# The weights of a two-layer block brought in in longer runs, four neighbouring rows to a partition

## The chip, the cores and the metric

The kernel runs on one core of one Trainium2 chip. The metric is the device time of one execution in microseconds; three runs of the kernel before are given below, and one further execution was taken with the hardware profiler.

## What is computed

A gated linear recurrence over 768 steps for 4 batches of 8 heads of 48 columns, and behind it a block of two matrix products with a gate between them:

```python
for t in range(S):                                  # S = 768, D = 48
    state = alpha[:, :, t, :, None] * state + np.einsum('bhd,bhe->bhde', k[:, :, t], v[:, :, t])
    y[:, :, t] = np.einsum('bhd,bhde->bhe', q[:, :, t], state)
x = y.transpose(0, 2, 1, 3).reshape(B * S, H * D)   # 3072 x 384
h = x @ w_in                                        # 384 x 2048
out = (h * np.cos(h)) @ w_out                       # 2048 x 384
```

Inputs and output are fp32; the kernel calculates its products in bf16. The change touches only how `w_in` and `w_out` lie in SBUF.

## The kernel before

The 3072 tokens are worked on in 12 pairs J of two 128-token chunks, three pairs to a batch. For each pair the recurrence is done in chunked form: logarithms of alpha (`ln`), their running sums by matmul (`cums0`, `cums`), exponentials (`icp`, `exps`), scaled k and q (`sk`, `sq`, into kh and qh), transposes (`trans`, into T_ps and qkT), scores, mask, the state between chunks (`outer`, `add`, `state`), and the transposed output (`yT`, evicted into xT). Then the two products follow. `m1` (`mlp1`) calculates h for four tiles of 128 of the 2048 middle columns at a time, u = 0 to 3, each tile f with three matmuls over the 384 rows of the first weights; `sin` makes the cosine on ACT and `gate` multiplies on DVE into gsb, where tile ft = 4u + f has its 128 middle columns on the partitions. `m2` (`mlp2`) sums gsb times the second weights over all 16 tiles, in four parts, into o_ps.

Both weights stay in SBUF for the whole kernel, as bf16: w1 with 128 partitions x 3 x 2048, w2 with 128 partitions x 16 x 384. They are brought in by eight transfers issued from POOL, which convert from fp32 on the way: `load_w1(u)` brings 512 columns, in runs of 2048 bytes of the source, and `load_w2(u)` brings 512 rows, in runs of 1536 bytes, row 128a + p of the block on partition p at place a. The inputs q, k, v and alpha are loaded by SP, and SP writes the results out. The loads of alpha of pair 2 wait for the last matmul of yT of pair 1 (`GATES` and `AFTER`), and all loads that stand behind it in SP's queue wait with it.

The order of all work is written out by hand: `PLAN` gives each step of each pair a planned time in ns, a step may name its engine (`:A`, `:D`), and the steps are issued sorted by these times. Only the order counts; each engine takes its own instructions in that order and waits where data is missing. `IDLE` puts in matmuls on zeros, "fillers", at some times in the start phase, so many at each.

Of the kernel before, what the change touches and what calls it, by code (L numbers as in the profile page):

```python
# [16 lines left out]
def kernel(  # L17
# [10 lines left out]
    nc = tc.nc  # L28
    B, H, S, D = q.shape
    DM, DF = moe_w_in.shape  # L30
    C = 128
# [8 lines left out]
    FW = 4  # L40
# [53 lines left out]
    w1 = consts.tile([C, KT, DF], BF, tag="w1", name="w1")  # L94
# [22 lines left out]

    WQ = FW * C

    def load_w1(u):  # L120
        nc.gpsimd.dma_start(
            out=w1[:, :, u * WQ : (u + 1) * WQ],
            in_=moe_w_in[:, u * WQ : (u + 1) * WQ].rearrange("(kk p) f -> p kk f", p=C),
        )

    def load_w2(u):
        nc.gpsimd.dma_start(
            out=w2[:, FW * u : FW * (u + 1)],
            in_=moe_w_out[u * WQ : (u + 1) * WQ, :].rearrange("(a p) d -> p a d", p=C),
        )  # L130

    act_now = [None]
# [221 lines left out]
    def mlp1(J, u):  # L354
        h_ps[J, u] = ps.tile([C, FW, T2], FP, tag="h", name="h_ps", bufs=3)
        for f in range(FW):
            ft = u * FW + f
            for kk in range(KT):
                nc.tensor.matmul(h_ps[J, u][:, f, :], w1[:, kk, ft * C : (ft + 1) * C], xT[J][:, kk, :],  # L359
                                 start=(kk == 0), stop=(kk == KT - 1))  # L360

    def cosine(J, u):
# [47 lines left out]
    def idle(n):  # L410
# [18 lines left out]


    PLAN = {
# [66 lines left out]
    }  # L498
    IDLE = [(1201, 12), (6413, 16), (11874, 2), (13039, 6), (14889, 9), (17476, 6)]

    order = []
    for key, line in PLAN.items():
        kind, *rest = key.split()
        for J, word in enumerate(line.split()):
            if word != "-":
# [39 lines left out]
```

## Time and profile before

| | |
|---|---|
| median of 3 runs | 187.04 us (187.01 to 188.32) |
| profiled execution | 186.2 us, of which its span is 184.4 us |
| granted TensorE clock | 1.00 |
| TensorE busy | 177.7 us, 96% of the span |
| VectorE, ScalarE, GpSimd busy | 72%, 69%, 45% |
| transfers of the first weights | 4 of 384 KB written, 7.6 us from issue to landing |
| transfers of the second weights | 4 of 384 KB written, 9.2 us |

In the lines of the profile, PE is TensorE's matmuls and PEld its weight loads, which run beside the matmuls; DVE is VectorE, ACT ScalarE, POOL GpSimd, SP the engine that issues most transfers. L359 is line 359 of the kernel before, the matmul of `mlp1`; L388 that of `mlp2`; L167 the matmul in `cums` with two moving columns; L121 and L127 are the two weight transfers. A group's line gives its tiles and shapes, the number of instructions, busy us, the mean ns of one, and behind the bar its engine's idle time before it and what ended that. A line of the waits gives who waited for whom, the us in total, how often, and the longest. A line of the chain gives start, length and what. Matmuls are pipelined, so the time from one to the next is read from the chain and not from the duration of one. In the DMA view a line of a queue gives packets, MB written and the time that its packets took as a share of all 16 DMA engines; q0 is POOL's queue, which carries the weights, and q1 is SP's.

### The profile page before, as it was taken

The page shows a single profiled execution, that of the slowest core. Times are in us where ns is not written, and L with a number is a line of the kernel's source. Part 1 is how long each engine was busy: PE and PEld are TensorE (multiplying, and loading weights), DVE is VectorE, ACT ScalarE, POOL GpSimd, SP SyncE. Part 2 cuts the span into 40 slices and gives each one's busy share as a digit, 9 for nine tenths or more (in the row PEclk, how much of TensorE's full clock was granted, in tenths as well). Part 3 has the DMA queues.
Part 4 walks back from the last instruction along what each step waited for, and adds up shares of the span by engine and source line. Part 5 has one row for each costly group of instructions (what it writes and reads, how often), then busy time and mean ns, then how long its engine had stood idle before and what let it go on. Part 6 is the DMA issues. An engine that isn't in the chain of part 4 may idle for free.

```text
span 184.4 us, 5780 instructions
## 1 busy us (share of the span) xinstructions
PE 177.7 (96%) x2478; PEld 127.1 (69%) x2480; DVE 132.6 (72%) x176; ACT 127.1 (69%) x166; POOL 83.9 (45%) x116
## 2 busy tenths in 40 slices
PE   7999999899999999999999999999999999999993
PEld 2455687565687776876778668676777786787772
DVE  7367673559889799899548986886979769352651
ACT  2572887899889987779787999637945163372720
POOL 5379830297765693943874189492600121000000
PEclk9999999999999999999999999999999999999999
DMA  5999999999999969968968893050420204010212
GB/s 148 261 261 192 187 203 247 237 271 264 257 197 242 310 174 279 226 158 202 301 151 211 202 304 72 0 132 14 116 73 4 60 5 170 4 43 4 85 43 85
DMA packets 60137, 29.47 MB, mean 160 GB/s; under 512 B 51024, under 2 KB 60112, under 8 KB 60112
## 3 DMA queue, kind: packets, MB, share of 16 engines
q1 hardware_dynamic: 56256, 25.86, 57.6%
q0 software_dynamic: 3712, 3.15, 11.1%
q8 instruction: 19, 0.31, 0.7%
q10 hardware_dynamic: 144, 0.10, 0.2%
q14 instruction: 6, 0.05, 0.1%
HBM read 25.17 MB, written 4.72 MB: 162 GB/s over the span
## 4 chain that ended last, share of the span: by engine, by line
PE 76%; ACT 10%; DMA 7%; DVE 2%; issue 1%; SPq 1%; ACTq 0%
PE h_ps L359 29%; PE o_ps L388 27%; DMA a<-in_alpha_dram 7%; PE y_ps L338 5%; PE A_ps L272 3%; PE T_ps L258 3%; PE idle_ps L414 3%; ACT lna L141 2%; DVE gsb L370 2%; PE U_ps L289 2%; ACT c_sb L365 2%; ACT xT L349 2%; PE o_last L382 1%; ACT L136 1%; ACT L365 1%
## 5 line engine op out<-in xcount | busy, mean ns | idle before, releaser
L370 DVE TENSOR_TENSOR gsb<-h_ps,c_sb 128x1024 bf16<-128x1024 f32 x48 | 58.1, 1221 | 24.1 <-ACT c_sb L365 23.2
L365 ACT ACTIVATE c_sb<-h_ps,halfpi 128x1024 bf16<-128x1024 f32 x48 | 53.1, 1115 | 23.5 <-PE h_ps L359 23.1
L359 PE MATMUL h_ps<-xT,w 128*128 128x256 bf16 x576 | 67.6, 273 | 0.6 <-DVE gsb L370 0.3
L388 PE MATMUL o_ps<-w,gsb 128*128 128x384 bf16 x368 | 66.5, 326 | 0.0
L359 PEld LDWEIGHTS <-w 128*128 128x128 bf16 x576 | 55.5, 98 | 9.5 <-issue 0.9
L388 PEld LDWEIGHTS <-gsb 128*128 128x128 bf16 x368 | 34.1, 98 | 20.7 <-issue 0.2
L277 DVE TENSOR_TENSOR A_sb<-A_ps,msk 128x1024 bf16<-128x1024 f32 x24 | 29.0, 1216 | 3.6 <-PE A_ps L272 3.6
L311 POOL TENSOR_TENSOR un<-us,c 128x384 bf16<-128x384 f32 x20 | 16.7, 837 | 30.0 <-DVE us L303 27.4
L212 POOL TENSOR_TENSOR kh<-k,icp 128x384 bf16<-128x384 f32 x22 | 21.8, 1002 | 14.6 <-ACT icp L192 14.6
L216 POOL TENSOR_TENSOR qh<-q,cp 128x384 bf16<-128x384 f32 x16 | 16.6, 1043 | 0.8 <-DMA q<-in_q_dram 0.8
L149 POOL TENSOR_TENSOR a<-a 128x384 f32<-128x384 f32 x9 | 9.0, 1000 | 15.7 <-DMA a<-in_alpha_dram 15.7
L264 DVE COPY qkT<-T_ps 128x1024 bf16<-128x1024 bf16 x18 | 11.8, 680 | 5.0 <-PE T_ps L258 4.8
L414 PE MATMUL idle_ps<-zeros 128*128 128x512 bf16 x49 | 12.9, 412 | 1.4 <-DVE zeros L52 1.2
L349 ACT CAST xT<-y_ps 128x384 bf16<-128x384 f32 x17 | 9.0, 599 | 5.6 <-PE y_ps L338 5.0
L219 POOL CAST vp<-v 128x768 bf16<-128x768 f32 x12 | 10.2, 854 | 5.7 <-DMA v<-in_v_dram 5.7
L141 ACT ACTIVATE lna<-a 128x768 bf16<-128x768 f32 x12 | 10.1, 843 | 3.5 <-DMA a<-in_alpha_dram 3.5
L136 ACT ACT_TABLE_LOAD x9 | 11.5, 1283 | 0.9 <-PEq L529 0.7
L365 ACT ACT_TABLE_LOAD x9 | 11.5, 1283 | 0.2
L303 DVE TENSOR_TENSOR us<-U_ps,un 128x384 f32<-128x384 f32 x16 | 8.7, 550 | 2.7 <-POOL un L311 2.5
L400 ACT COPY o_sb<-o_ps 128x384 f32<-128x384 f32 x11 | 5.2, 476 | 7.2 <-PE o_ps L388 7.2
L414 PEld LDWEIGHTS <-zeros 128*128 128x128 bf16 x51 | 4.8, 105 | 7.3 <-issue 2.2
L264 ACT COPY qkT<-T_ps 128x1024 bf16<-128x1024 bf16 x6 | 6.0, 1014 | 5.3 <-PE T_ps L258 5.1
(70 smaller groups left out, 159.7 us busy)
## 6 DMA issues: line engine op xcount, KB each, us to landing
a<-in_alpha_dram SPq DMA_DIRECT2D x12, 384.0 KB, 5.9
q<-in_q_dram SPq DMA_DIRECT2D x12, 384.0 KB, 5.7
k<-in_k_dram SPq DMA_DIRECT2D x12, 384.0 KB, 5.9
v<-in_v_dram SPq DMA_DIRECT2D x12, 384.0 KB, 5.6
out_dram<-o_sb SPq DMA_DIRECT2D x23, 192.0 KB, 3.0
vs<-vp SPq DMA_DIRECT2D x36, 64.0 KB, 2.9
w<-in_moe_w_in_dram POOLq DMA_DIRECT2D x4, 384.0 KB, 7.6
w<-in_moe_w_out_dram POOLq DMA_DIRECT2D x4, 384.0 KB, 9.2
```

The source lines that it names most:

```text
L136: nc.scalar.preload_act_table_set("natural_log_exp_and_others")
L141: nc.scalar.activation(out=lna_t[J % NL][:, :, :, 0:D].rearrange("p e h d -> p h e d"), in_=a_sb.pop(J), func=AF.Ln)
L212: eng.tensor_tensor(out=kh_t[J % NQ][:, e, :, 0:D], in0=kqv["k", J][:, :, e], in1=icp_, op=ALU.mult)
L216: eng.tensor_tensor(out=qh_t[J % NQ][:, e, :, 0:D], in0=kqv["q", J][:, :, e], in1=cp, op=ALU.mult)
L264: copy(out=qkT_sb[J][:, c], in_=T_ps[J][:, c].rearrange("r n e s -> r n (e s)"))
L277: nc.vector.tensor_tensor(out=A_sb[J][:, c].rearrange("s a p t -> s (a p) t"), in0=A_ps.pop((J, c)).rearrange("s a p t -> s (a p) t"), in1 ...
L311: nc.gpsimd.tensor_tensor(out=u, in0=U_sum.pop(n), in1=c2_sb[J][:, :, c].unsqueeze(3).to_broadcast([C, NP, 2, D]), op=ALU.mult)
L359: nc.tensor.matmul(h_ps[J, u][:, f, :], w1[:, kk, ft * C : (ft + 1) * C], xT[J][:, kk, :], start=(kk == 0), stop=(kk == KT - 1))
L365: nc.scalar.activation(out=c_sb[J, u], in_=h_ps[J, u], func=AF.Sin, bias=halfpi, scale=1.0)
L370: nc.vector.tensor_tensor(out=gsb[J][:, u * FW : (u + 1) * FW], in0=h_ps.pop((J, u)), in1=c_sb.pop((J, u)), op=ALU.mult)
L388: nc.tensor.matmul(o_ps[J, c][:, 0:DM], gsb[J][:, ft, c * C : (c + 1) * C], w2[:, ft], start=(ft == 0), stop=(ft == NF - 1))
L414: nc.tensor.matmul(idle_ps[0], zeros[:, 0:C], zeros, start=True, stop=True)
```

## The change

The second weights lie otherwise in SBUF: of each block of 512 rows, partition p now takes the four neighbouring rows 4p to 4p + 3, which is one run of 6144 bytes of the source. So that gsb's partitions fit to it, tile f of block u must hold the middle columns 4c + f of the block, c = 0 to 127, and the weight loads of L359 read the columns of w1 four apart. The first weights keep their place in SBUF and are brought in by two transfers of 1024 columns, in runs of 4096 bytes; the steps "w1" 2 and 3 are empty. `PLAN` has new times and one of the fillers is gone.

```diff
     def load_w1(u):
-        nc.gpsimd.dma_start(
-            out=w1[:, :, u * WQ : (u + 1) * WQ],
-            in_=moe_w_in[:, u * WQ : (u + 1) * WQ].rearrange("(kk p) f -> p kk f", p=C),
-        )
+        if u < 2:
+            cols = slice(2 * u * WQ, 2 * (u + 1) * WQ)
+            nc.gpsimd.dma_start(out=w1[:, :, cols], in_=moe_w_in[:, cols].rearrange("(kk p) f -> p kk f", p=C))

     def load_w2(u):
         nc.gpsimd.dma_start(
             out=w2[:, FW * u : FW * (u + 1)],
-            in_=moe_w_out[u * WQ : (u + 1) * WQ, :].rearrange("(a p) d -> p a d", p=C),
+            in_=moe_w_out[u * WQ : (u + 1) * WQ, :].rearrange("(p a) d -> p a d", a=FW),
         )
...
     def mlp1(J, u):
         h_ps[J, u] = ps.tile([C, FW, T2], FP, tag="h", name="h_ps", bufs=3)
         for f in range(FW):
-            ft = u * FW + f
             for kk in range(KT):
-                nc.tensor.matmul(h_ps[J, u][:, f, :], w1[:, kk, ft * C : (ft + 1) * C], xT[J][:, kk, :],
+                cols = w1[:, kk, u * WQ : (u + 1) * WQ].rearrange("p (c a) -> p a c", a=FW)[:, f]
+                nc.tensor.matmul(h_ps[J, u][:, f, :], cols, xT[J][:, kk, :],
                                  start=(kk == 0), stop=(kk == KT - 1))
...
-        "w1": "13130 11430 15880 12280",
-        "w2": "19161 17541 20961 22950",
+        "w1": "11430 12280 13180 13181",
+        "w2": "18455 16835 20255 22800",
...
-    IDLE = [(1201, 12), (6413, 16), (11874, 2), (13039, 6), (14889, 9), (17476, 6)]
+    IDLE = [(1201, 12), (6413, 16), (11874, 2), (13039, 6), (14889, 8), (17327, 6)]
```

The other times of `PLAN` are new as well, mostly by less than 1 us. Engine by engine, the order of the instructions is the same as before except for two things: POOL issues six weight transfers instead of eight, and TensorE has one filler fewer, ahead of the transposes T_ps of pair 1.

128 rows, old and new, of the table PLAN are left out of this document.

## The prediction, made before the changed kernel was run

> **What bounds the kernel now.** I read the page's busy shares first, then the chain that ended last, then the waits, and then went into the one stretch in which the weights are brought in.
>
> ```profile
> PE 177.7 (96%) x2478; PEld 127.1 (69%) x2480; DVE 132.6 (72%) x176; ACT 127.1 (69%) x166; POOL 83.9 (45%) x116
> PEclk9999999999999999999999999999999999999999
> ```
> TensorE is busy for 177.7 of 184.4 us at the full clock; no other engine is above 72%. A busy share can hide stalls inside, so the waits of TensorE alone, from 20 us to 181.5 us, are the better measure:
>
> ```profile
> PE cums_h L155 <- ACT lna L141: 0.8, 1, 0.8
> PE T_ps L258 <- DVE gsb L370: 0.3, 1, 0.3
> PE h_ps L359 <- DVE gsb L370: 0.3, 1, 0.3
> ```
> That is all: 1.4 us in 161 us. Behind 20 us nothing that makes another engine or a transfer quicker can bring more than 1.4 us. What can cost much is anything that makes a matmul slower, since there is no idle time to take it up. The chain in order of time shows the pace of the two sorts of matmul that matter (start, length, what), first in the start phase and then late:
>
> ```profile
> 26.71 6.89 DMA a<-in_alpha_dram
> 33.60 0.02 issue
> 33.62 0.85 ACT lna L141
> ...
> 98.41 0.08 PE cums L167 x4
> ...
> 148.44 3.93 PE h_ps L359 x36
> ```
> 36 matmuls of L359 take 3.93 us: 109 ns each, for 256 columns. Four of L167 take 0.08 us: 20 ns each, and eight in another place 0.18 us, 23 ns each. L167 streams 2 columns behind a full 128x128 weight load, so a full load from consecutive columns holds up the matmul behind it for no more than about 23 ns. The first line is the only transfer on the chain behind 10 us: the load of the third pair's alpha, which is held back to the end of yT of pair 1 and then needs 6.89 us.
>
> **The change, part by part.**
>
> *1. The weight loads of L359 read every fourth column.* 576 loads that read 256 bytes of a partition in one run now pick 128 columns out of 1024 bytes. The trace has no strided weight load. The nearest rows are these (all loads of TensorE by shape):
>
> ```profile
> L359 PEld LDWEIGHTS <-w 128*128 128x128 bf16 x576 | 55.5, 98 | 9.5 <-issue 0.9 <-DVE gsb L370 0.2
> L338 PEld LDWEIGHTS <-vs 128*32 128x32 bf16 x384 | 6.0, 97 | 0.0
> L234 PEld LDWEIGHTS <-ident_bf 64*64 64x64 bf16 x12 | 0.7, 103 | 0.9 <-issue 0.5
> ```
> All records are near 98 ns, whether 32 or 128 columns are read, so a record is mostly a latency that the next matmul does not wait out; what counts is the 23 ns. Lower bound: the stride costs nothing (a gain is excluded, because the matmul behind is already at its streaming pace of 109 ns). Upper bound for a load that is still pipelined: four times the stretch read, four times the time, 4 x 23 = 92 ns. A load runs under the 256-column matmul before it, and 92 is below 109, so within a group of 12 both bounds give 0. They differ at the first load of a group. Of the 48 groups, 13 follow o_ps (163 ns a matmul, hidden) and 22 follow another group of L359; the other 13 follow short matmuls of 20 to 41 ns, and there a load may show by up to 92 - 23 = 69 ns: 13 x 69 = 0.9 us. I take twice the consecutive price, 46 ns, since half of what is read is the nearer case to the row: 13 x 23 = +0.3 us, range 0 to +0.9.
>
> A rule of the Trainium skill bears on it (SBUF — State Buffer, the note on cachelines in the section Door 1: The DMA port swizzle): accesses that hit the same 16-byte line twice or more run at full bandwidth, and each crossing to a new line pays a penalty whose size is not given. Four bf16 columns are 8 bytes, so each line is still hit twice and by the first half the load is free, by the second it crosses four times as often; no row here shows which, and the sum by the first half would be 0.3 us lower.
>
> *2. First weights in two transfers, not four; the second weights in longer runs.* The DMA engines are full from 14 us to 30 us with weights alone (two windows of the DMA view, 14 to 30 us and 30 to 34 us):
>
> ```profile
> DMA packets 3655, 3.13 MB, mean 196 GB/s; under 512 B 181, under 2 KB 3652, under 8 KB 3652
> q0 software_dynamic: 3584, 3.06, 123.9%
> ...
> q1 hardware_dynamic: 2617, 0.99, 98.9%
> q0 software_dynamic: 120, 0.08, 13.4%
> ```
> 3.06 MB of bf16 in 16 us is 191 GB/s written, twice that read as fp32, and the loads of the next pair (q1) flow only once the weights (q0) have drained. By the windows, 14 to 22 us (mostly first weights, 2048-byte runs) moved 186 GB/s and 22 to 30 us (mostly second weights, 1536-byte runs) 205 GB/s. The longer run is not the faster one, so the run's length is not what limits, and I expect little: bounds are no change and the whole at 205 GB/s, which ends 8 x (1 - 186/205) = 0.7 us earlier. A loss is not excluded: at 158 GB/s, near the lowest slices of the window, 1.57 MB of first weights would take 10.0 us, about 1.5 us more than now. I take half the gain, 0.35 us. What is it worth? The alpha load lands at 33.60, but ACT is free for it only at 33.55, when the table load that ends at 32.27 + 1.28 us is over. So from this alone 0.05 us.
>
> *3. POOL.* Two issues of 0.8 us each (L121: 2.47 us for three, 0.80 for the fourth) go away, one ahead of the kh product at 13.85 us and one ahead of the un product at 16.58 us; the second weights keep four issues. POOL's kh and qh of pair 1 end 0.8 us earlier. They feed T_ps at 17.03 us, which sits behind fillers on TensorE in any case, so this is worth nothing by itself; it lets the next part through.
>
> *4. One filler matmul fewer.* The order on each engine is otherwise the same: SP, ACT and DVE keep theirs, TensorE loses one of nine idle matmuls ahead of T_ps, 1.90 us / 9 = 0.21 us.
>
> ```profile
> 16.88 0.15 issue
> 17.03 0.64 PE T_ps L258 x32
> ```
> T_ps can start at 16.82: its last input on DVE, qh, ends at 15.56 + 0.67 = 16.23 us, and POOL's at 15.0. From there to the matmuls at 21.28 us the chain is TensorE and ACT, so yT of pair 1 and ACT's table load come 0.21 us earlier. The weights must keep up: quarter 1 is wanted at 21.1 us, quarter 0 at 22.8, quarter 3 at 24.1. Before, the fourth quarter landed at 15.75 + 7.9 = 23.65 us; the second half, which holds quarters 2 and 3, lands then or a little earlier, so 0.4 us is left. If it lands 1 us late, 0.6 us is lost. The alpha load is no help to ACT if it does not land earlier too: with the 0.35 us of part 2 it lands at 33.25 and ACT is ready at 33.34, so 0.21 + 0.05 = 0.26 us is kept, without it nothing. I take -0.25 us.
>
> **The sum.** +0.3 - 0.25 = about 0 (from -0.3 to +0.9 with the likely bounds, +2 with slower transfers). Against the profiled execution, 184.4 us of span and 1.8 us around it, 186.2 us in all, this gives 186.2. The median of the three runs, 187.04, is 0.8 us higher than that execution, so the forecast for a median is 187.0 us. A measurement of this kernel tells about 1% (1.9 us) from no change, which is not reached.
>
> **The rivals.**
>
> *A. Strided loads outgrow their cover (slower).* The place is the background load under each L359 matmul; it decides from 109 ns on, and from there each nanosecond costs 576 ns over the kernel, or 0.49 us where L359 lies on the chain (29% of 184.4 = 53.5 us of its 576 x 109 ns = 62.8 us, 85%). If strided loads are no longer pipelined, a load takes its record of 98 ns and the 69 ns of the longer stretch: 167 ns, 58 ns too many, 58 x 0.49 = +28 us: 215 us. A load only just too long, at 118 ns, gives +4.4 us: 191.4. For it: nothing in the trace shows a strided load, TensorE has no slack, and 92 ns is my guess of a bound. Against it: 86 ns of room over the 23 ns shown. The skill's penalty for each line crossed, named above, is the mechanism that would do it.
>
> *B. Longer runs are slower or the second half is late (slightly slower).* At 158 GB/s the weights end 1.5 us later, the alpha load too, and quarter 3 stalls its matmuls by up to 0.9 us, part of the same delay: +1.5 to +2: 188.5 to 189. For it: the 2048-byte runs move less than the 1536-byte ones. Against it: fewer, longer packets.
>
> *C. The transfers become much quicker (faster).* Then alpha of pair 2 lands well ahead, but ACT is not free earlier than 33.34 us, and all waits of TensorE behind 20 us are 1.4 us. With the filler the most is 1.6 us, 185.4; ACT's order lets through 0.3 us, 186.7. What speaks against much quicker transfers is that 205 GB/s written is 410 GB/s read, the most of the windows read here. The Trainium skill (DMA: Bandwidth & Descriptors, section Bandwidth) advises transfers of 1 MiB and more, which the halves are and the quarters are not; by it the weights would drain sooner, and the time would be the 186.7 us just given.
>
> *D. It does nothing that counts:* all loads hidden, transfers at their old rate: 187.0, inside the forecast.
>
> **Chances and range.** Forecast with D and the mild ends of B and C: 0.64. A: 0.24, spread from 189 to 240. B over 1%: 0.05. C or a gain from elsewhere over 1%: 0.07. So faster 0.07, same 0.64, slower 0.29. The range takes the forecast's own (186.0 to 188.4), C to 185.4, and A up to a load that is 10 ns too long: 185.4 to 191.5.
>
> **What would show it.** Right: the L359 matmuls at 109 ns in the chain, their loads at 98 to 170 ns in the record, TensorE's waits behind 20 us near 1.4 us, weights drained by about 30 us, T_ps at 16.8 us. Wrong: an L359 group of 36 taking more than 4.1 us (rival A; 28 us more would be 6 us a group), L359 waiting for a weights transfer near 24 us (B), or the wait of cums_h on ln growing above 0.8 us.

## The result and the profile after

The changed kernel takes 187.89 us in the median of 20 runs (187.57 to 190.47), the kernel before 186.78 us in 20 runs beside them. The ratio of the fast runs (one run of the changed kernel, 190.47 us, counts as slow and is left out) is 1.0075, 95% interval 1.0052 to 1.0099. That is slower by 1.4 us in the mean; the medians are 1.1 us apart. It lies inside the stated range and inside 1%, but it is not "no change", which was forecast: the loss is clear of noise.

The page of the changed kernel, busy shares and the clock:

```profile
PE 177.9 (96%) x2477; PEld 133.6 (72%) x2479; DVE 132.5 (71%) x176; ACT 127.1 (68%) x166; POOL 81.8 (44%) x114
PEclk9999999999999999999999999999999999999999
```
Its span is 185.9 us against 184.4. TensorE's busy time grew by 0.2 us only, so nearly all of the 1.5 us is idle time. The waits of TensorE from 20 us on show where:

```profile
PE h_ps L360 <- DMA w<-in_moe_w_in_dram: 1.6, 1, 1.6
PE cums_h L156 <- ACT lna L142: 0.8, 1, 0.8
PE T_ps L259 <- DVE gsb L371: 0.3, 1, 0.3
PE h_ps L360 <- DVE gsb L371: 0.3, 1, 0.3
```
The last three are the waits of before, to the digit. The first is new: one wait for the first weights, 1.6 us. The timeline of TensorE (start, length, what, and in brackets the idle time ahead) puts it in its place, and the chain shows what follows:

```profile
21.23 0.27 PE L360 MATMUL h_ps<-xT,w 128*128 128x256 bf16 x1
23.13 1.39 PE L360 MATMUL h_ps<-xT,w 128*128 128x256 bf16 x11 [1.63 <-DMA w<-in_moe_w_in_dram]
```
```profile
12.44 10.64 DMA w<-in_moe_w_in_dram
...
35.36 0.85 ACT lna L142
...
39.31 0.32 PE cums L156
```
The first matmul of the second stage runs at 21.23 us (21.28 before). The second one waits until 23.13, though it belongs to the same quarter of the columns. From there all is late: ln of the third pair at 35.36 instead of 33.62 us, the running sums of the fourth at 39.31 instead of 37.58. From that point to the end of the span it is 146.6 us, before 146.8. So the whole loss is made between 21.2 and 23.1 us, once, and nothing behind it is slower. The first half, which holds the quarter that is read, was issued at 11.5 us and landed 7.9 us later, at 19.4 us; the transfer that ends at 23.1 us is the second half.

The weight loads did change, and it costs nothing there:

```profile
L360 PEld LDWEIGHTS <-w 128*128 128x128 bf16 x576 | 62.1, 114 | 5.0 <-DMA w<-in_moe_w_in_dram 1.9 <-issue 0.4 <-DVE gsb L371 0.2
```
A strided load's record is 114 ns instead of 98, and late in the kernel 36 matmuls still take 3.93 us.

The program itself names what is waited for. These are the weight loads of `mlp1` that wait for a weight transfer (DMASW, numbered in the order of issue; the other names are waits for engines, and the number in front is the place in the listing), first in the kernel before, then in the changed one:

```
507 L359 Ldweights w_134 [waits PE_49,DMASW0_49]
535 L359 Ldweights w_134 [waits DMASW2_49]
559 L359 Ldweights w_134 [waits DVE_49,DMASW1_49]
695 L359 Ldweights w_134 [waits DMASW3_49]

505 L360 Ldweights w_134 [waits PE_49,DMASW0_49]
507 L360 Ldweights w_134 [waits DMASW1_49]
```
Before, each quarter is waited for by the first load that reads it. Afterwards the very next load behind the first one, which reads quarter 1 in the second row tile, waits for the second half, which it does not read. These waits stand in the program, so they were put in when the kernel was built; the chip only keeps to them. In w1 a partition holds three row tiles of 2048 columns. The second half is written to columns 1024 to 2047 of each, that is to elements 1024 to 6143 with gaps. The first load reads elements 512 to 1023, ahead of that stretch; the second begins at element 2560, inside it, in a gap.

### The profile page after: what moved, and what is told of

It is laid out like the page before. It is cut to its first block, busy times and chain, and to the rows that moved or that the text cites. A ratio compares the mean times of both kernels' runs of the same rounds, so it can differ in the third digit from the quotient of the medians.

```text
span 185.9 us, 5774 instructions
## 1 busy us (share of the span) xinstructions
PE 177.9 (96%) x2477; PEld 133.6 (72%) x2479; DVE 132.5 (71%) x176; ACT 127.1 (68%) x166; POOL 81.8 (44%) x114
## 4 chain that ended last, share of the span: by engine, by line
PE 71%; ACT 11%; DMA 9%; DVE 3%; SPq 2%; issue 1%; POOL 1%; ACTq 0%
PE h_ps L360 30%; PE o_ps L389 27%; DMA w<-in_moe_w_in_dram 6%; PE y_ps L339 4%; DMA v<-in_v_dram 3%; ACT c_sb L366 3%; PE A_ps L273 3%; DVE gsb L371 3%; PE T_ps L259 2%; ACT L137 2%; SPq L105 2%; PE U_ps L290 2%; ACT lna L142 2%; PE o_last L383 1%; ACT L366 1%; ACT icp L193 1%
## 5 line engine op out<-in xcount | busy, mean ns | idle before, releaser
L360 PEld LDWEIGHTS <-w 128*128 128x128 bf16 x576 | 62.1, 114 | 5.0 <-DMA w<-in_moe_w_in_dram 1.9
L137 ACT ACT_TABLE_LOAD x9 | 11.5, 1283 | 0.9 <-PEq L530 0.7
L366 ACT ACT_TABLE_LOAD x9 | 11.5, 1283 | 0.2
L273 PE MATMUL A_ps<-qkT 48*128 48x128 bf16 x192 | 9.5, 218 | 0.0
```

The costliest lines, as they stand in the source:

```text
L137: nc.scalar.preload_act_table_set("natural_log_exp_and_others")
L273: nc.tensor.matmul(A_ps[J, c][:, a, p, :], qkT[r, c, NP + p, :], qkT[r, c, p, :], start=True, stop=True)
L360: nc.tensor.matmul(h_ps[J, u][:, f, :], cols, xT[J][:, kk, :], start=(kk == 0), stop=(kk == KT - 1))
L366: nc.scalar.activation(out=c_sb[J, u], in_=h_ps[J, u], func=AF.Sin, bias=halfpi, scale=1.0)
```

## The experiments

**Theory 1**: where a read is strided, it is taken to collide with everything between the first and the last element of a transfer, gaps included, while a consecutive read is told apart exactly. **Theory 2**: a transfer of twice the size lands later, and the data that is read is really not there at 21.2 us. **Theory 3**: strided weight loads cost time on TensorE.

**Halves in two tiles**

```diff
-    w1 = consts.tile([C, KT, DF], BF, tag="w1", name="w1")
+    w1 = [consts.tile([C, KT, DF // 2], BF, tag=f"w1_{b}", name=f"w1_{b}") for b in range(2)]
...
-            nc.gpsimd.dma_start(out=w1[:, :, cols], in_=...)
+            nc.gpsimd.dma_start(out=w1[u], in_=...)
...
-                cols = w1[:, kk, u * WQ : (u + 1) * WQ].rearrange(...)[:, f]
+                cols = w1[u // 2][:, kk, u % 2 * WQ : (u % 2 + 1) * WQ].rearrange(...)[:, f]
```


> The changed kernel with the first weights in two tiles of their own, one for each half, everything else the same. Theory 1 (a strided weight load is taken to touch the whole stretch that the other half's transfer spans, so the second weight load waits for a half that it does not read): the wait of 1.6 us of h_ps on w is gone, the first 12 matmuls of L360 run from 21.2 us without a break, the span is 184.1 to 184.6 us, ratio to before 0.995 to 1.002. Theory 2 (the half that is read lands at 23.1 us, because a transfer of twice the size lands later): the wait stays at 1.6 us, ratio about 1.008. Theory 3 (the strided loads cost time on TensorE): the wait may go, but the ratio stays above 1.004.

Measured: 187.04 us against 186.54, ratio 1.0022 (1.0001 to 1.0043), just above what theory 1 gave. The waits of TensorE behind 20 us:

```profile
PE h_ps L360 <- issue: 1.4, 1, 1.4
PE cums_h L156 <- ACT lna L142: 0.8, 1, 0.8
PE T_ps L259 <- DVE gsb L371: 0.3, 1, 0.3
PE h_ps L360 <- DVE gsb L371: 0.3, 1, 0.3
```
The wait on the transfer is gone, the matmuls of the second stage run from 21.00 us without a break, and the sums of the fourth pair start at 37.26 us. But this profiled execution has another wait of 1.4 us, which ends near 97 us and for which the profile shows no releaser. With it the span is 185.3 us instead of the 184.1 to 184.6 that were expected. The median of the 12 runs is close to this execution's 187.12 us, so the wait is probably not rare in this kernel; its cause is open (last section).

**Halves side by side in one tile**

```diff
-    w1 = consts.tile([C, KT, DF], BF, tag="w1", name="w1")
+    w1 = consts.tile([C, 2, KT, DF // 2], BF, tag="w1", name="w1")
...
-            nc.gpsimd.dma_start(out=w1[:, :, cols], in_=...)
+            nc.gpsimd.dma_start(out=w1[:, u], in_=...)
...
+                cols = w1[:, u // 2, kk, u % 2 * WQ : (u % 2 + 1) * WQ].rearrange(...)[:, f]
```


> The changed kernel with one tile for the first weights, but ordered half, row tile, column, so that each half is one stretch of 6144 bytes a partition. Theory 1 in the form that the span of the transfer from its first to its last byte counts: no wait, as with two tiles, ratio 0.995 to 1.002. If it were the tile as a whole that counts once a strided access is in it: the wait of about 1.6 us stays, ratio about 1.008. Theory 2: the wait stays.

Measured: 186.19 us against 186.54, ratio 0.9996 (0.9974 to 1.0018), span 184.1 us. Waits:

```profile
PE cums_h L156 <- ACT lna L142: 0.8, 1, 0.8
PE T_ps L259 <- DVE gsb L371: 0.3, 1, 0.3
PE h_ps L360 <- DVE gsb L371: 0.3, 1, 0.3
```
One tile, the same transfers, the same strides: only the gaps between the pieces of a transfer are gone, and with them the wait. So it is the span of the transfer, from its first to its last element, and neither the tile nor the landing time. Theory 2 falls: the half that is read had landed.

**Two halves, consecutive columns**

```diff
-                cols = w1[:, kk, u * WQ : (u + 1) * WQ].rearrange("p (c a) -> p a c", a=FW)[:, f]
+                cols = w1[:, kk, u * WQ + f * C : u * WQ + (f + 1) * C]
```
and the second weights laid out as before.

> The changed kernel's two transfers of the first weights and its order of work, but consecutive columns in the weight loads and the second weights laid out as before (1536-byte runs). Theory 1: consecutive reads are told apart exactly, so no wait on the second half at 21 us, span 184.1 to 184.7 us, ratio 0.995 to 1.002, weight loads of 98 ns. Theory 2: the wait of about 1.6 us stays, ratio about 1.008. Theory 3: ratio 0.995 to 1.002, since no load is strided.

Measured: 186.55 us, ratio 1.0007 (0.9986 to 1.0027), no wait on w, loads of 98 ns. With gaps in the transfer but consecutive reads there is no false wait, as theory 1 says.

**The layout alone, four transfers, one tile** (the kernel before with the strided read and the second weights four rows a partition)

> The kernel before (its four transfers of the first weights, its plan and fillers) with only the layout edit: columns four apart, second weights four rows a partition. Theory 1: the first weight load waits for quarters 1 and 0 (the latter lands near 21.6 us), the second for quarters 3 and 2 (near 23.6 us), though it reads quarter 1 alone, which landed near 17.6 us; some 2.2 us of waiting of h_ps on w, span about 186.4 us, ratio 1.008 to 1.015. Theory 2: no wait, since the transfers are those of before, ratio 0.997 to 1.003. Theory 3: no wait, ratio about 1.007.

Measured: 189.18 us in 6 runs, ratio 1.016 (1.0121 to 1.0199), a little more than expected. Its first load waits for quarters 0 and 1, the second one for 2 and 3, as expected. Its timeline:

```profile
22.17 0.27 PE L360 MATMUL h_ps<-xT,w 128*128 128x256 bf16 x1
23.78 2.51 PE L360 MATMUL h_ps<-xT,w 128*128 128x256 bf16 x11 [1.34 <-DMA w<-in_moe_w_in_dram]
```
The second load reads quarter 1, which landed near 17.8 us, and starts when quarter 2 has landed, at 23.65 us. With the transfers of before the stride alone brings the wait: theory 1 again, and against theory 2. Behind the wait the matmuls start 213 ns apart instead of 109, at a granted clock of 0.68 from 22 to 27 us (0.50 from 24.7 to 26.7). This execution (190.50 us) is one of two whose mean clock is 0.988 and 0.990; the other four, at 0.998 or more, take 188.45 to 189.39 us, which is 1.010 to 1.015 times the median of the kernel before, as expected.

**The same with each quarter in a tile of its own**

```diff
-    w1 = consts.tile([C, KT, DF], BF, tag="w1", name="w1")
+    w1 = [consts.tile([C, KT, FW * C], BF, tag=f"w1_{b}", name=f"w1_{b}") for b in range(4)]
...
+            out=w1[u],
...
+                cols = w1[u][:, kk].rearrange("p (c a) -> p a c", a=FW)[:, f]
```


> The kernel before with the layout edit alone (columns four apart, second weights four rows a partition), as in the run with quarters and strides, but each quarter of the first weights in a tile of its own. If the span of the transfers is all that made that run wait: no wait of h_ps on w, span 184.0 to 184.8 us, ratio 0.995 to 1.003, 2.5 us less than the same kernel with one tile. If the strided loads or the longer runs cost something by themselves: ratio above 1.004 with no such wait.

Measured: 186.67 us against 186.81, ratio 0.9995 (0.9974 to 1.0017), span 184.3, no wait on w. The false wait, with the low clock behind it, is the whole difference to the kernel with one tile. Strided loads and longer runs cost nothing that can be measured (theory 3 falls), and two transfers bring no more than four.

**Columns eight and sixteen apart**, one execution each

> Both weights laid out eight apart: columns of a half 8c + f, second weights eight rows a partition, halves in two tiles. For the price of the stride alone. The record of a weight load is 98 ns at step 1 and 114 at step 4. If the price goes with the stretch that is read: 98 + 16 x 7/3 = 135 ns. If each column that starts a new 16-byte line costs the same: about 130 ns, and no more at sixteen. In both cases the matmuls stay at 109 ns.

> Both weights laid out sixteen apart, one tile, so that the first matmul needs both halves (a wait of about 2 us on w is due to the data and is no part of the question). The record of a weight load: by the stretch 98 + 16 x 15/3 = 178 ns, by lines the same as eight apart. The matmuls stay at 109 ns unless a load holds up the next matmul by more than that.

Measured: 186.67 and 188.5 us, a single execution each; the second holds the wait that was announced, 2.2 us. The groups of the weight loads, first eight, then sixteen apart:

```profile
L360 PEld LDWEIGHTS <-w 128*128 128x128 bf16 x576 | 64.0, 144 | 2.5 <-issue 0.4
```
```profile
L360 PEld LDWEIGHTS <-w 128*128 128x128 bf16 x576 | 63.9, 145 | 4.9 <-issue 3.0 <-DVE gsb L371 0.2
```
98, 114, 144, 145 ns for steps of 1, 4, 8 and 16: at these four steps the price rises until each column lies in a 16-byte piece of its own (eight bf16 columns) and then stays, so it does not go with the stretch that is read (178 ns at sixteen). Both forecasts for eight, 135 and 130, were too low. The 16 bytes are the line that the Trainium skill describes (SBUF — State Buffer, Door 1: The DMA port swizzle). The sentence of the Trainium skill there that eight bf16 columns apart are still free does not agree: that step has the full price. At four apart, where a piece of 16 bytes still holds two of the columns that are read, the record is already 16 ns longer. Late in both kernels 36 matmuls take 3.93 us as ever. By the starts of single matmuls in the traces, the cost shows only at the second matmul of a group that follows short ones: behind L167 it starts 109 ns after the first at step 1, 117 at step 4 and 147 at step 8; in five other places 119, 136 and 167. Each of these is a mean of the places. At step 4 that is 4 x 8 + 5 x 17 = 117 ns in the whole kernel.

**Fewer fillers, halves side by side** (twice, on two chips)

```diff
-    IDLE = [..., (14889, 8), (17327, 6)]
+    IDLE = [..., (14889, 4), (17327, 6)]
```


> The kernel with the halves side by side, and four of the eight fillers ahead of T_ps of pair 1 taken out (4 x 0.21 = 0.85 us). If POOL's two issues saved let T_ps start earlier: its last input, qh on DVE, is there at 16.3 us, T_ps starts at 16.1 to 16.4 us instead of 17.0, the third pair's ln is 0.5 to 0.8 us earlier where alpha has landed by then, ratio to before 0.994 to 0.998. If alpha's landing takes its place as the bound: less than 0.3 us, ratio 0.998 to 1.001. The rival is that a shorter run of fillers lowers the granted clock: below 1.00 behind 16 us, ratio above 1.002.

> The kernel with the halves side by side and four fillers instead of eight once more, on the same chip as the kernel before with fewer fillers, so that the two can be set side by side. Ratio to before 0.992 to 0.997 if the first measurement holds; the difference to the kernel before with fewer fillers is what the weights' new layout is worth once the false wait is gone: 0 to 0.7 us.

Measured: 186.03 us against 186.81, ratio 0.9941 (0.9915 to 0.9966), and 185.77 against 186.71, ratio 0.9954 (0.9929 to 0.998). This version beats both kernels. In the first of the two profiled executions ln of pair 2 starts at 33.67 us, no earlier than before; the table below shows why that is no contradiction.

**Fewer fillers in the kernel before** (five instead of nine)

> The kernel before with five fillers instead of nine ahead of T_ps of pair 1, nothing else. For whether the gain of the same edit in the kernel with the halves side by side (ratio 0.994) needs the weights' change. If POOL's earlier kh and qh and the earlier end of the weights are what lets it through: T_ps is held by qh on POOL, which ends at 15.8 us, and DVE's at 16.2, so it starts at 16.3, but ln of pair 2 is held by alpha's landing at 33.6 us; ratio 0.998 to 1.001. If the fillers alone held the start phase: ratio 0.993 to 0.997, as there.

Measured: 186.02 us, ratio 0.9979 (0.9958 to 1.0), as expected for a kernel that alpha's landing holds. The start of ln of pair 2 on ACT, first this kernel, then the one with the halves side by side on the same chip:

```profile
31.30 1.28 ACT L136 ACT_TABLE_LOAD   x1
33.47 0.84 ACT L141 ACTIVATE lna<-a 128x768 bf16<-128x768 f32 x1 [0.88 <-DMA a<-in_alpha_dram]
```
```profile
31.27 1.28 ACT L137 ACT_TABLE_LOAD   x1
32.57 0.84 ACT L142 ACTIVATE lna<-a 128x768 bf16<-128x768 f32 x1
```
Both are ready at 32.6 us. Without the new transfers ACT then waits 0.88 us for alpha, which stands behind the old weights; with them it does not. TensorE itself also waits there for the second weights, 0.6 us, which it does not with the new transfers. In the traces the new transfers are thus worth 0.9 us at this point, once the fillers no longer cover it. In the medians the two kernels are 0.25 us apart, with intervals that overlap, so as a time it is not shown. The spans of the two profiled executions differ by 0.4 us; the one with the halves side by side has a wait "issue" of 0.5 us of its own near 96 us.

Starts in single executions must be set side by side with care, because the start phase is not equally long in all of them: T_ps of pair 0 begins between 10.76 and 11.95 us. The table gives the starts in us by the timelines; the last column is the way from T_ps of pair 0 to ln of pair 2.

| kernel (fillers ahead of T_ps of pair 1) | T_ps of pair 0 | T_ps of pair 1 | ln of pair 2 | from first to last |
|---|---|---|---|---|
| before (9) | 10.87 | 17.03 | 33.62 | 22.75 |
| changed (8) | 11.02 | 16.97 | 35.36 | 24.34 |
| two tiles (8) | 10.79 | 16.74 | 33.30 | 22.51 |
| halves side by side (8) | 11.07 | 17.02 | 33.58 | 22.51 |
| before, fewer fillers (5) | 10.76 | 16.06 | 33.47 | 22.71 |
| side by side, fewer fillers (4), first | 11.95 | 17.03 | 33.67 | 21.72 |
| side by side, fewer fillers (4), second | 10.79 | 15.88 | 32.57 | 21.78 |

The two executions with four fillers agree once the start phase is taken off: ln comes 1.0 us earlier than before.

## Why the prediction was wrong

**The bound** was read rightly: TensorE had 1.4 us of waits behind 20 us, nothing gained more, and the 1.6 us of wait that was added to them showed as 1.4 us of time.

**Part 4 is the step that failed**: "The weights must keep up: quarter 1 is wanted at 21.1 us, quarter 0 at 22.8, quarter 3 at 24.1", with the second half landing at 23.65 us and "0.4 us is left". The times of landing held (the second half was there at 23.1). What failed is who waits for whom. I let each matmul wait for the half that it reads. The order of the instructions, which I compared, had stayed; their waits had not, and I did not compare those. The second half was wanted at 21.3 us, not at 24.1, so 0.4 us to spare became 1.6 us of wait. Rival B had the second half late, but at the wrong matmul, and priced it at up to 0.9 us.

**The filler and the landing of alpha** (-0.25): this term was right and the wait hid it. T_ps of pair 1 began at 16.97 us (forecast 16.82), but this execution's start phase was 0.15 us longer; counted from T_ps of pair 0 it came 5.95 us later instead of 6.16, the 0.21 us of one filler. Where the wait is gone, with two tiles and with the halves side by side, ln of pair 2 comes 0.24 us earlier by the last column of the table. In the changed kernel the alpha load mattered to nothing, since ACT came later still. With the halves side by side the ratio is 0.9996 (0.9974 to 1.0018), which fits the "about 0" of the sum; the interval is too wide to show 0.1 us more or less.

**Part 1** (+0.3, 0 to +0.9) had the right sign and was too large: 0.12 us by the single starts. 46 ns was taken for the load, 23 more than a consecutive one; what a group start pays is 8 to 17 ns, at nine groups and not 13, and at the second load of a group and not the first. Rival A did not happen, nor at sixteen apart. (The upper end of the range was meant for a load 10 ns too long; at 0.49 us for each nanosecond that is 191.9 us and not 191.5.)

**Part 2**: of the weights 0.08 MB were still moving between 30 and 34 us, now 0.01 MB, and 14 to 22 us moved 194 GB/s instead of 186; the expected half gain fits. **Part 3** held: POOL's kh and qh of pair 1 ended 0.6 us earlier, 0.75 us counted from T_ps of pair 0 (forecast 0.8). The second weights' issues fell from 0.8 to 0.6 us, which I had left at 0.8.

## What to carry to other kernels

When a change makes a read strided or cuts a transfer anew, compare the waits of the two programs and not only the order: a read with a step can be held to a transfer that writes around it. Lay out a tile so that each transfer fills one stretch of a partition, or give each transfer its own tile, and the false wait is gone; side by side and in four tiles this had no cost that could be measured (ratios 0.9996 and 0.9995). A gain can lie idle behind something that was tuned to the old state; here 0.9 us at one point came out only when fillers ahead of it were taken away.

## What was not expected of the hardware

In the profiled run of the layout with four transfers the granted clock was 0.68 from 22 to 27 us, behind TensorE's wait of 1.34 us, and the matmuls started 213 ns apart. In that execution the wait cost about its own length once more: 11 matmuls, each some 100 ns longer. It need not: behind the waits of 1.63 us in the changed kernel, 2.17 us with columns sixteen apart and 1.40 us with two tiles, the profiled executions show a clock of 1.00. What decides is open. The changed kernel may do the same in part of its executions, though none of those was profiled: four of its 20 runs have a mean clock of 0.990 or 0.991 and take 189.25 to 190.47 us, the other 16 have 0.997 or more and take 187.57 to 188.74.

The wait of 1.4 us "issue" in the run with two tiles lies in a stretch (94 to 98 us) where the loads of v and a 16 KB transfer of instructions (q8) share DMA engines that are nearly full. The second execution with four fillers has a wait "issue" of 0.5 us at the same place, 95.4 to 95.9 us, also with such a transfer of instructions between 92 and 96 us; the one with columns eight apart has the transfer (92 to 97 us) but no such wait. That the instructions came late is a guess; no run tested it.
